# Loads of one batch with six in flight, and three smaller edits, in a gated linear attention fused with a ReGLU layer

## The chip, the cores and the metric

The kernel runs on one core of a Trainium2 chip. The metric is the device time of one execution in microseconds (us), as the median of several runs. The profiled execution is a separate run; its span, from the first to the last instruction, is a little shorter than the device time.

## The reference

Inputs q, k, v and f_logit have 4 batches, 8 heads, 768 positions and a head width of 48, in float32. The first half is a recurrence along the sequence, for each batch and head:

```
f = 1 / (1 + exp(-f_logit))
for t in range(768):
    state = f[t, :, None] * state + outer(k[t], v[t])     # 48 x 48
    y[t]  = q[t] @ state
```

The results of the heads are put side by side to a matrix x of 3072 x 384, and the second half is a feed-forward layer:

```
out = (relu(x @ w_gate) * (x @ w_val)) @ w_out            # 384 -> 1536 -> 384
```

## The kernel before

**Chunks.** The sequence is cut into 6 steps (c = 0 to 5) of 128 positions, and a step has 4 batches (b = 0 to 3). Within a step the recurrence becomes matrix products. For one batch of one step, from step 1 on, the work is this:

- `f_in` is loaded; ScalarE makes ln(1 + exp(-f)) of it in two passes, for two batches at a time (lines 572 and 575, the second writes `bneg`). So this pair of instructions needs the f of both batches.
- `cum` on TensorE: line 582 multiplies with a triangle of ones, which gives running sums of log decay; line 584 adds four one-column products that give the decay over the whole step. ScalarE makes `expo` of the sums (lines 591 and 593), and `dec` of the four columns (line 597, not in the last step).
- GpSimd multiplies k and q by `expo` into `hats` (lines 602 and 605) and turns v into `vpad` (line 558).
- `hats` is transposed into `qkT`: in steps 1 and 2 by TensorE (line 615, then a copy on VectorE, line 621), from step 3 on by a DMA that transposes (line 624).
- `scores` on TensorE (line 638), the mask on VectorE (line 644), the output products on TensorE (lines 673 and 677), a copy to `xn` on ScalarE (line 691). `xn` is transposed into `xT`: by TensorE (line 699, copy on VectorE, line 703) in steps below `first_xbar_x`, by a DMA (line 707) from there on.
- `state` (lines 718, 732 and 734) carries the state to the next step.

**Feed-forward.** For each step, line 766 makes the gate and value products for 12 blocks of hidden columns, 773 and 777 the ReLU and the product, line 789 the output product, 809 the copy to `osb`, and 812 the store.

**Who orders the work.** The kernel lists its operations with estimated durations and dependences, and a list scheduler (`Plan.schedule`) simulates the five engines and the DMA. At each turn it takes the operation that can start first, by priority where several can. The result is a fixed order of instructions on each engine; at run time each instruction waits for semaphores in that order. So an estimate that is off does not change the order: the engine stands and waits. Feed-forward products have a priority value 1000 higher than the attention's, so they are taken only where the plan sees no attention work ready. All loads, stores and transposing DMAs are issued by SyncE (SP) and stand in one order too.

**Loads.** `early` lists the loads of steps 0 and 1 and of the weights. From step 2 on a loop adds the loads in the order f, k, q, v for each group of `load_batches` batches. Each must wait until the load `flight` places earlier has landed:

```
for b in range(0, B, load_batches):
    for n in "fkqv":
        ...
        loads.append(load(n, c, b, b + load_batches, loads[-flight:][:1]))
```

A batch of one tensor and step is 192 KB, in rows of 192 bytes, so a load of two batches is 384 KB. The tiles for the loads are kept three times (`NL = 3`), so the loads of step c need the buffers of step c - 3.

Of the kernel before, what the change touches and what calls it, by code (L numbers as in the profile page):

```python
# [43 lines left out]
class Plan:  # L44
# [9 lines left out]
    def add(self, eng, emit, reads=(), writes=(), occ=0.5, lat=0.2, prio=0, opens=(), after=(), follows=(),  # L54
            paced=()):
        op = Op(eng, emit, list(reads), list(writes), occ, lat, prio, opens, after, follows, paced)
        op.idx = len(self.ops)
        self.ops.append(op)
        return op
# [169 lines left out]
def bass_hgrn2_outer__then__ffn_reglu_kernel(  # L229
# [13 lines left out]
             "wo2 f1.2.4 k1.2.4 q1.2.4 v1.2.4").split()  # L243
    lag = 4.0
    first_xbar_qk = 3
    flight = 3
    WP = 0
    NWARM = 100
    split_first = 1
# [1 line left out]
    spread_engines = ['ACT', 'DVE', 'ACT', 'ACT']  # L251
    load_engine = 'SP'
    n_tiled = 1
    first_xbar_x = 4
    load_batches = 2
    hat_engines = ['DVE', 'POOL']
    TAIL = [0, 256, 384]
    groups = [(0,0,4,1),(1,0,2,0),(1,2,4,0),(2,0,4,0),(3,0,4,0),(4,0,4,0),(5,0,4,0)]
    B, H, S, D = q.shape
    C = 128  # L260
    NC = S // C
    HD = H * D
# [3 lines left out]
    NP = H // 2  # L266
# [10 lines left out]
    bneg = [sb(f"bneg{i}", [128, 2, H, 64], BF16) for i in range(NB)]  # L277
# [168 lines left out]
    def chain(line, *args, **kw):  # L446

        last = tails.get(line)
        tails[line] = add(*args, follows=[last] if last else [], **kw)
        return tails[line]  # L450
# [95 lines left out]
    def attention(c, b):  # L546
# [14 lines left out]
        if c == 0:  # L561
            if b % 2 == 0:
                first_pair(b // 2)
            khat = khn[b % 2]
            kh_key = [f"khn{b % 2}"]
            back_transpose(b)
        else:
            parts = [(b, b + 2)] if b % 2 == 0 else []
            for b0, b1 in parts:
                fl = fin[:, b0:b1, :, :].rearrange("p b h d -> p (b h) d")  # L570
                keys = [f"f{li}_{x}" for x in range(b0, b1)]
                add("ACT", lambda: sc.activation(fl, fl, AF.Exp, scale=-1.0), keys, keys, prio=P,  # L572
                    **act_t((b1 - b0) * HD))
                bo = bneg[bi][:, b0 % 2:b0 % 2 + b1 - b0, :, 0:D].rearrange("p b h d -> p (b h) d")
                add("ACT", lambda: sc.activation(bo, fl, AF.Ln, bias=1.0), keys + [f"bneg{bi}"],
                    [f"bn{bi}_{x % 2}" for x in range(b0, b1)], prio=P, **act_t((b1 - b0) * HD))

            bn = bneg[bi][:, bj, :, :]
            bc = Bank("bc")

            def cum():
                te.matmul(bc.ap[:, 0:HD], tri[:, :], bn[:, :, 0:D])  # L582
                for p in range(NP):
                    mm = te.matmul(bc.ap[:, HD + p:HD + p + 1],  # L584
                                   bn[:, 2 * p:2 * p + 2, :].rearrange("p h d -> p (h d)"), ones[:, :])
                return mm
            chain("cum", "PE", cum, ["tri", "ones", f"bneg{bi}", f"bn{bi}_{bj}"], [bc], occ=0.29, lat=PE_L,
                prio=P, opens=[bc])

            ex = expo[ei]  # L590
            add("ACT", lambda: sc.activation(ex[:, 1, :], bc.ap[:, 0:HD], AF.Exp, scale=1.0), [bc],  # L591
                [f"expk{ei}"], prio=P + 1, **act_t(HD))
            add("ACT", lambda: sc.activation(ex[:, 0, :], bc.ap[:, 0:HD], AF.Exp, scale=-1.0), [bc],  # L593
                [f"expq{ei}"], prio=P + 1, **act_t(HD))
            if c < NC - 1:
                for j in range(2):
                    add("ACT", lambda lo=64 * j, j=j: sc.activation(dec[ai][lo:lo + 64, :, j], bc.ap[lo:lo + 64, HD:HD + NP],
                                                                    AF.Exp, scale=-1.0),
                        [bc, f"dec{ai}"], [f"dec{ai}_{j}"], prio=P + 2, **act_t(NP))

            hq, hk = hats[hi][:, 0, :, 0:D], hats[hi][:, 1, :, 0:D]
            add("POOL", lambda: gp.tensor_tensor(hk, kin[:, b, :, :], ex[:, 1, :].rearrange("p (h d) -> p h d", h=H),  # L602
                                                 ALU.mult),
                [f"k{li}_{b}", f"expk{ei}", f"hats{hi}"], [f"hk{hi}"], prio=P + 2, occ=0.95, lat=0.2)
            add("POOL", lambda: gp.tensor_tensor(hq, qin[:, b, :, :], ex[:, 0, :].rearrange("p (h d) -> p h d", h=H),  # L605
                                                 ALU.mult),
                [f"q{li}_{b}", f"expq{ei}", f"hats{hi}"], [f"hq{hi}"], prio=P + 2, occ=0.95, lat=0.2)
            if c < first_xbar_qk:
                tp = Bank("tp")

                def transposes():
                    t16 = tp.ap[:, :].bitcast(BF16)
                    for x in (1, 0):
                        for p in range(NP):
                            mm = te.transpose(t16[:, (x * NP + p) * C:(x * NP + p + 1) * C],  # L615
                                              hats[hi][:, x, 2 * p:2 * p + 2, :].rearrange("p h d -> p (h d)"), ident[:])
                    return mm
                chain("transposes", "PE", transposes, ["ident", f"hk{hi}", f"hq{hi}"], [tp], occ=pe_t(*[C] * 8), lat=PE_L, prio=P + 3,
                    opens=[tp])
                flat = qkT[qi].rearrange("p x n t -> p (x n t)")  # L620
                add("DVE", lambda: ve.tensor_copy(flat, tp.ap[:, :].bitcast(BF16)),
                    [tp], qk_key, prio=P + 4, **dve_t(512))
            else:
                op = add("SP", lambda: sy.dma_start(qkT[qi].rearrange("p x n t -> p (x n) t"),
                                                    hats[hi][:, :, :, :].rearrange("p x h d -> p (x h d)"), transpose=True),
                         [f"hk{hi}", f"hq{hi}"], qk_key, prio=P + 3, occ=1.2, lat=1.2)
                dma(op, f"qkT{qi}", 1.06, late)
                op.ring = "own" if load_engine == "ACT" else "SP"
            khat = hats[hi][:, 1, :, :].rearrange("p h d -> p (h d)")
            kh_key = [f"hk{hi}", f"hats{hi}"]  # L630
# [149 lines left out]
    def ffn_out(g, *bs):  # L780

        gi = g % NG
        cuts = TAIL if (g, bs[-1]) == (NC - 1, B - 1) else [0, DM]
        parts = [(b, n0, n1, Bank("f")) for b in bs for n0, n1 in zip(cuts, cuts[1:])]

        def proj_out(o, b, s, n0, n1):
            def run():
                for j in range(s * OJ, (s + 1) * OJ):
                    mm = te.matmul(o.ap[:, 0:n1 - n0], gT[gi][:, j, b * C:(b + 1) * C], wo[:, j, n0:n1],  # L789
                                   start=(j == 0), stop=(j == NJ - 1))  # L790
                return mm
            return run

        def rows(b, n0, n1, o, s):
            js = range(s * OJ, (s + 1) * OJ)
            P = (g + 1) * B * 10 + 5 + NJ * 3 + b * 3
            chain("ffn", "PE", proj_out(o, b, s, n0, n1), [f"gT{gi}_{j}_{b}" for j in js] + sorted({f"wo{j // WJ}" for j in js}),
                  [o], occ=pe_t(*[n1 - n0] * OJ), lat=PE_L, prio=P + 1000, opens=[o] if s == 0 else [])
        if len(cuts) > 2:
            for part in parts:  # L800
                for s in range(NJ // OJ):
                    rows(*part, s)
        else:
            for s in range(NJ // OJ):
                for part in parts:
                    rows(*part, s)
        for b, n0, n1, o in parts:
            oi, P = (g * B + b) % NO, (g + 1) * B * 10 + 5 + NJ * 3 + b * 3
            add("ACT", lambda o=o, oi=oi, n0=n0, n1=n1: sc.activation(osb[oi][:, n0:n1], o.ap[:, 0:n1 - n0], AF.Copy), [o], [f"osb{oi}_{x}" for x in TAIL[:-1] if n0 <= x < n1],  # L809
                prio=P, **act_t(n1 - n0))  # L810
            dst = bass.AP(tensor=out.tensor, offset=(b * S + g * C) * DM + n0, ap=[[DM, C], [1, n1 - n0]])
            op = add("SP", lambda dst=dst, oi=oi, n0=n0, n1=n1: sy.dma_start(dst, osb[oi][:, n0:n1]), [f"osb{oi}_{x}" for x in TAIL[:-1] if n0 <= x < n1], [f"out{g}_{b}_{n0}"],
                     occ=0.2, lat=0.9, prio=P)
            dma(op, f"osb{oi}_{n0}", 0.45 * (n1 - n0) / DM)

    OJ = 4
    OPAIR = 2
    count = {"h": 0}
# [44 lines left out]
                n += 1  # L863
            op.val = n

    stores = [op for op in order["SP"] if op.writes and op.writes[0].startswith("out")]

    def run(name, eng):
        for op in order[name]:
# [63 lines left out]
```

## Time and profile before

| what | value |
|---|---|
| device time | median of 3 runs 203.14 us (202.06 to 204.03) |
| span of the profiled run | 201.4 us |
| TensorE busy | 191.7 us, 95% of the span |
| ScalarE, VectorE, GpSimd busy | 115.2, 107.9 and 77.3 us |
| bytes moved by DMA | 31.35 MB, 156 GB/s over the span |
| DMA issues of loads after step 1 | 32 of 384 KB |
| DMA issues that transpose | 12 of qkT, 8 of xT |

The page gives the busy share of each engine in 40 slices of about 5 us. The chain of waits follows the work that ended last back from the last instruction. The view of windows gives busy time, the granted TensorE clock and the share of the DMA engines in stretches that one chooses; a share above 1 means that packets of several transfers lay over each other. The timeline of SP shows its DMA issues; such an issue contains its own wait for semaphores[...].

### The profile page before, as it was taken

How to read it: one execution, taken by the hardware profiler on the slowest of the kernel's cores; microseconds unless marked ns; L12 is line 12 of the kernel's file. 1: busy time of each engine (PE TensorE's matmuls, PEld its weight loads, DVE VectorE, ACT ScalarE, POOL GpSimd, SP SyncE). 2: the span in 40 equal slices, each digit the busy share in tenths (PEclk: the TensorE clock that was granted, in tenths of full speed). 3: DMA queues.
4: the chain of work that ended last, by engine and by line, in shares of the span. 5: the costliest groups of instructions: out<-in, count | busy, mean ns of one | idle time of the engine just before them, and what ended most of it. 6: DMA issues, size and time to landing. Idle time of an engine off the chain costs nothing.

```text
span 201.4 us, 4570 instructions
## 1 busy us (share of the span) xinstructions
PE 191.7 (95%) x1813; PEld 124.4 (62%) x1813; DVE 107.9 (54%) x212; ACT 115.2 (57%) x264; POOL 77.3 (38%) x111
## 2 busy tenths in 40 slices
PE   7989899799999999999999999599999999999995
PEld 5766688676789787855664655245555555444564
DVE  7268575565098988628586846135462334433210
ACT  2976868716678686877677572744354333443412
POOL 5189203563559687772858364053000000000000
PEclk9999999999999999999999999969999999999999
DMA  4999999999999999999989998979222001111113
GB/s 119 234 223 196 198 200 180 204 231 210 230 232 232 158 247 189 221 198 230 192 161 234 159 199 186 189 156 221 77 63 59 24 19 39 39 39 42 39 39 117
DMA packets 116660, 31.35 MB, mean 156 GB/s; under 512 B 109600, under 2 KB 116640, under 8 KB 116640
## 3 DMA queue, kind: packets, MB, share of 16 engines
q1 hardware_dynamic: 112656, 27.53, 67.2%
q0 software_dynamic: 3984, 3.54, 11.0%
q8 instruction: 14, 0.23, 0.5%
q14 instruction: 6, 0.05, 0.1%
HBM read 25.95 MB, written 4.72 MB: 152 GB/s over the span
## 4 chain that ended last, share of the span: by engine, by line
PE 73%; DMA 13%; SPq 8%; ACT 2%; POOL 2%; issue 1%; DVE 0%
PE ps L766 37%; PE ps L789 22%; SPq L399 7%; DMA q_in<-in_q_dram 4%; DMA wv<-in_moe_w_val_dram 4%; PE ps L638 3%; DMA f_in<-in_f_logit_dram 3%; DMA v_in<-in_v_dram 3%; PE ps L615 2%; PE ps L677 2%; PE ps L582 2%; PE ps L673 2%; PE ps L718 1%; PE ps L699 1%; PE ps L584 1%
## 5 line engine op out<-in xcount | busy, mean ns | idle before, releaser
L777 DVE TENSOR_TENSOR gT<-relu,ps 128x256 bf16<-128x256 bf16 (+1 forms) x96 | 52.2, 552 | 59.9 <-PE ps L766 37.2
L766 PE MATMUL ps<-xT,wg 128*128 128x256 bf16 (+1 forms) x288 | 63.1, 328 | 0.3 <-DMA wg<-in_moe_w_gate_dram 0.3
L773 ACT ACTIVATE relu<-ps 128x256 bf16<-128x256 f32 (+1 forms) x96 | 46.3, 490 | 29.1 <-PE ps L766 28.7
L766 PE MATMUL ps<-xT,wv 128*128 128x256 bf16 (+1 forms) x288 | 62.6, 326 | 0.0
L789 PE MATMUL ps<-wo,gT 128*128 128x384 bf16 (+2 forms) x300 | 52.5, 320 | 0.0
L789 PEld LDWEIGHTS ps<-wo,gT 128*128 128x128 bf16 x300 | 27.7, 98 | 17.4
L766 PEld LDWEIGHTS ps<-xT,wg 128*128 128x128 bf16 x288 | 27.0, 98 | 15.6 <-DMA wg<-in_moe_w_gate_dram 0.6
L644 DVE TENSOR_TENSOR ptm<-ps,tri 128x512 bf16<-128x512 f32 x48 | 30.6, 684 | 10.8 <-PE ps L638 10.7
L766 PEld LDWEIGHTS ps<-xT,wv 128*128 128x128 bf16 x288 | 26.1, 98 | 16.0 <-ACT relu L773 0.2
L809 ACT ACTIVATE osb<-ps 128x384 f32<-128x384 f32 (+2 forms) x25 | 11.8, 477 | 30.6 <-PE ps L789 30.5
L602 POOL TENSOR_TENSOR hats<-k_in,expo 128x384 bf16<-128x384 f32 x20 | 20.0, 1000 | 20.3 <-ACT expo L591 20.3
L605 POOL TENSOR_TENSOR hats<-q_in,expo 128x384 bf16<-128x384 f32 x20 | 20.0, 1002 | 2.2 <-DMA q_in<-in_q_dram 2.2
L734 POOL TENSOR_TENSOR st<-ssum,dec 128x384 bf16<-128x384 f32 x16 | 13.3, 830 | 16.2 <-DVE ssum L732 16.2
L455 PE MATMUL ps<-zeros 128*128 128x256 bf16 x89 | 13.0, 301 | 1.1 <-DVE zeros L359 1.1
L691 ACT ACTIVATE xn<-ps 128x384 bf16<-128x384 f32 x20 | 9.8, 488 | 7.1 <-PE ps L677 7.1
L558 POOL CAST vpad<-v_in 128x384 bf16<-128x384 f32 x24 | 12.0, 515 | 3.0 <-DMA v_in<-in_v_dram 2.8
L572 ACT ACTIVATE f_in<-f_in 128x768 f32<-128x768 f32 x10 | 8.4, 838 | 6.4 <-DMA f_in<-in_f_logit_dram 6.4
L591 ACT ACTIVATE expo<-ps 128x384 f32<-128x384 f32 x20 | 9.8, 492 | 3.0 <-PE ps L584 2.9
L455 PEld LDWEIGHTS ps<-zeros 128*128 128x128 bf16 x89 | 9.0, 107 | 3.0 <-DVE zeros L359 1.1
L638 PE MATMUL ps<-qkT 48*128 48x128 bf16 x192 | 8.9, 226 | 1.2 <-ACT qkT L528 0.8
L593 ACT ACTIVATE expo<-ps 128x384 f32<-128x384 f32 x20 | 10.0, 498 | 0.0
L732 DVE TENSOR_TENSOR ssum<-ps,st 128x384 f32<-128x384 f32 x16 | 8.8, 551 | 1.1 <-PE ps L718 0.9
(71 smaller groups left out, 158.3 us busy)
## 6 DMA issues: line engine op xcount, KB each, us to landing
out_dram<-osb SPq DMA_DIRECT2D x23, 192.0 KB, 2.2
f_in<-in_f_logit_dram SPq DMA_DIRECT2D x10, 384.0 KB, 6.2
k_in<-in_k_dram SPq DMA_DIRECT2D x10, 384.0 KB, 6.4
q_in<-in_q_dram SPq DMA_DIRECT2D x10, 384.0 KB, 4.5
v_in<-in_v_dram SPq DMA_DIRECT2D x10, 384.0 KB, 4.8
wg<-in_moe_w_gate_dram POOLq DMA_DIRECT2D x3, 384.0 KB, 7.1
wv<-in_moe_w_val_dram POOLq DMA_DIRECT2D x3, 384.0 KB, 7.4
wo<-in_moe_w_out_dram POOLq DMA_DIRECT2D x3, 384.0 KB, 7.2
```

What stands on the lines that cost most here:

```text
L399: op = add(eng, lambda: e.dma_start(dst, src), [], [f"{n}{c % NL}_{b}" for b in range(b0, b1)], occ=(0.8 if eng == "SP" else 0.3) * (b1 - ...
L455: op = add("PE", lambda: te.matmul(cold.ap[:, 0:256], zeros[:, 0:128], zeros[:, :]), ["zeros"], [cold], occ=0.22 if i < 17 else 0.11, lat= ...
L558: add("POOL", lambda: gp.tensor_copy(vout, vin[:, b, :, :].rearrange("p (n j) d -> p n j d", j=2)), [f"v{li}_{b}", f"vpad{vi}"], [f"v_{vi} ...
L602: add("POOL", lambda: gp.tensor_tensor(hk, kin[:, b, :, :], ex[:, 1, :].rearrange("p (h d) -> p h d", h=H), ALU.mult), [f"k{li}_{b}", f"ex ...
L605: add("POOL", lambda: gp.tensor_tensor(hq, qin[:, b, :, :], ex[:, 0, :].rearrange("p (h d) -> p h d", h=H), ALU.mult), [f"q{li}_{b}", f"ex ...
L638: mm = te.matmul(s.ap[:, p * C:(p + 1) * C], qkT[qi][lo:lo + D, 1, p, :], qkT[qi][lo:lo + D, 0, p, :])
L644: add("DVE", lambda j=j, s=s: ve.tensor_tensor(ptm[mi][:, j, :, :], s.ap[:, :].rearrange("p (n t) -> p n t", n=NP), mask, ALU.mult), [s, " ...
L734: add("POOL", lambda: gp.tensor_tensor(t4(s_new), t4(tmp), rate, ALU.mult), [key] + dk, [f"S{b}_{c % 2}"], prio=P + 8, **pool_t(HD))
L766: mm = te.matmul(bank.ap[:, 0:n], wt[:, kt, j * 128:(j + 1) * 128], xT[xi][:, kt, n0:n1], start=(kt == 0), stop=(kt == NK - 1))
L773: add("ACT", lambda: sc.activation(relu[ri][:, 0:n], gate.ap[:, 0:n], AF.Relu), [gate], [f"relu{ri}"], prio=P, **act_t(n))
L777: add("DVE", lambda: ve.tensor_tensor(gT[gi][:, j, n0:n1], relu[ri][:, 0:n], val.ap[:, 0:n], ALU.mult), [val, f"relu{ri}"], [f"gT{gi}_{j}_ ...
L789: mm = te.matmul(o.ap[:, 0:n1 - n0], gT[gi][:, j, b * C:(b + 1) * C], wo[:, j, n0:n1], start=(j == 0), stop=(j == NJ - 1))
```

## The change

Four constants or conditions change what the kernel does; the rest of the diff adds options that keep their old meaning (`STORE = 'SP'` leaves the stores where they were, and `first_stores` is empty).

- `load_batches` 2 to 1: from step 2 on a load brings one batch (192 KB). The order becomes f, k, q, v of batch 0, then of batch 1, and so on.
- `flight` 3 to 6: a load waits for the one six places earlier, so that again six batches at most are under way. It is to keep the DMA evenly busy with smaller pieces.
- `first_xbar_x` 4 to 3: the four transposes of x in step 3 move from TensorE and VectorE to DMAs on SP.
- In step 5 the four one-column products of `cum` are left out, since no later step uses the decay. The plan's estimate for `cum` is lowered by 0.12 there.

```diff
-    flight = 3
+    flight = 6
...
-    first_xbar_x = 4
-    load_batches = 2
+    first_xbar_x = 3
+    load_batches = 1
     hat_engines = ['DVE', 'POOL']
+    STORE = 'SP'
...
             def cum():
-                te.matmul(bc.ap[:, 0:HD], tri[:, :], bn[:, :, 0:D])
-                for p in range(NP):
+                mm = te.matmul(bc.ap[:, 0:HD], tri[:, :], bn[:, :, 0:D])
+                for p in range(NP if c < NC - 1 else 0):
                     mm = te.matmul(bc.ap[:, HD + p:HD + p + 1],
                                    bn[:, 2 * p:2 * p + 2, :].rearrange("p h d -> p (h d)"), ones[:, :])
                 return mm
-            chain("cum", "PE", cum, ["tri", "ones", f"bneg{bi}", f"bn{bi}_{bj}"], [bc], occ=0.29, lat=PE_L,
+            chain("cum", "PE", cum, ["tri", "ones", f"bneg{bi}", f"bn{bi}_{bj}"], [bc], occ=0.29 - (0.12 if c == NC - 1 else 0), lat=PE_L,
                 prio=P, opens=[bc])
...
-            op = add("SP", lambda dst=dst, oi=oi, n0=n0, n1=n1: sy.dma_start(dst, osb[oi][:, n0:n1]), [f"osb{oi}_{x}" for x in TAIL[:-1] if n0 <= x < n1], [f"out{g}_{b}_{n0}"],
-                     occ=0.2, lat=0.9, prio=P)
+            op = add(STORE, lambda dst=dst, oi=oi, n0=n0, n1=n1: (sy if STORE == "SP" else sc).dma_start(dst, osb[oi][:, n0:n1]), [f"osb{oi}_{x}" for x in TAIL[:-1] if n0 <= x < n1], [f"out{g}_{b}_{n0}"],
+                     follows=first_stores if g == 0 else [], occ=0.2 if STORE == "SP" else 0.4, lat=0.9 if STORE == "SP" else 1.2, prio=P)
```

More of the change, by code (lines that the diff above doesn't have):

```diff
@@ L811, in ffn_out @@
             dst = bass.AP(tensor=out.tensor, offset=(b * S + g * C) * DM + n0, ap=[[DM, C], [1, n1 - n0]])
-            op = add("SP", lambda dst=dst, oi=oi, n0=n0, n1=n1: sy.dma_start(dst, osb[oi][:, n0:n1]), [f"osb{oi}_{x}" for x in TAIL[:-1] if n0 <= x < n1], [f"out{g}_{b}_{n0}"],
-                     occ=0.2, lat=0.9, prio=P)
+            op = add(STORE, lambda dst=dst, oi=oi, n0=n0, n1=n1: (sy if STORE == "SP" else sc).dma_start(dst, osb[oi][:, n0:n1]), [f"osb{oi}_{x}" for x in TAIL[:-1] if n0 <= x < n1], [f"out{g}_{b}_{n0}"],
+                     follows=first_stores if g == 0 else [], occ=0.2 if STORE == "SP" else 0.4, lat=0.9 if STORE == "SP" else 1.2, prio=P)
             dma(op, f"osb{oi}_{n0}", 0.45 * (n1 - n0) / DM)
+    first_stores = [tails["loadSP"]] if '0' == "1" else []
     OJ = 4
@@ L864, in bass_hgrn2_outer__then__ffn_reglu_kernel @@
             op.val = n
-    stores = [op for op in order["SP"] if op.writes and op.writes[0].startswith("out")]
+    stores = [op for op in order[STORE] if op.writes and isinstance(op.writes[0], str) and op.writes[0].startswith("out")]
     def run(name, eng):
```

## The prediction

> **What bounds the kernel now.** I read the 40 slices first: they show whether TensorE (PE) has holes.
>
> ```profile
> PE   7989899799999999999999999599999999999995
> ...
> PEclk9999999999999999999999999969999999999999
> DMA  4999999999999999999989998979222001111113
> ```
>
> PE is full from slice 8 (40 us) to the end, but for one slice, number 25 (126 to 131 us), with a 5. In the slice after it the granted clock is at 6. The DMA engines are about full until slice 26. So PE sets the time, and the DMA stands close behind it for the first 136 us. The part up to 40 us (loads of steps 0 and 1 and of the weights) belongs to lines that the change does not touch, so I leave it as it is. The windows around the hole come next; columns are the window, its length, PE, PEld, DVE, ACT and POOL busy, the granted clock, the DMA share and GB/s.
>
> ```profile
> 116.00:122.00 6.00, 5.71 (x59) 3.08 (x55) 3.13 (x5) 3.34 (x8) 4.46 (x5) 1.00 1.01 215
> 122.00:127.00 5.00, 5.00 (x46) 2.74 (x45) 2.10 (x4) 1.09 (x2) 1.09 (x3) 1.00 0.68 129
> 127.00:130.00 3.00, 0.81 (x8) 0.29 (x7) 0.69 (x1) 2.73 (x6) 0.00 (x0) 1.00 1.33 229
> 130.00:135.00 5.00, 5.00 (x40) 2.52 (x39) 1.25 (x2) 3.21 (x8) 2.08 (x3) 0.66 0.94 194
> ```
>
> PE is idle 2.19 us in 127 to 130. After that 5 us run at a mean clock of 0.66, which costs 0.34 x 5 = 1.7 us. Just before, in 122 to 127, the DMA was at 0.68 and 129 GB/s: it had too little to do, right before PE waited for a load. The chain of waits says which load.
>
> ```profile
> 118.80 0.61 ACT relu L773
> 119.42 1.22 SPq L812
> 120.68 1.19 SPq L707
> ...
> 121.92 5.33 DMA f_in<-in_f_logit_dram
> 127.27 0.84 ACT f_in L572
> ...
> 128.98 0.74 ACT bneg L575
> ...
> 129.76 0.34 PE ps L582
> ```
>
> This is f of batches 2 and 3 of step 5, the last of the f loads. It is issued at 121.92, lands 5.33 us later, goes through two ScalarE passes, and `cum` (line 582) stands first in PE's order. PE has 60 us of feed-forward products left, but behind that instruction. Why was it issued so late? SP's timeline:
>
> ```profile
> 115.71 2.42 SPq L624 DMA_TRANSPOSE qkT<-hats  x1
> 118.17 0.58 SPq L399 DMA_DIRECT2D v_in<-in_v_dram  x1
> 118.80 1.84 SPq L812 DMA_DIRECT2D out_dram<-osb  x1
> 120.68 1.19 SPq L707 DMA_TRANSPOSE xT<-xn  x1
> 121.92 0.58 SPq L399 DMA_DIRECT2D f_in<-in_f_logit_dram  x1
> ```
>
> SP's order puts it behind a transpose, a store (1.84 us, with a wait for ScalarE) and another transpose. The limit of three in flight did not hold it: SP waits for loads to land for 1.3 us in all between 40 and 140 us. What holds it is its place in the order, which comes from the plan, where the limit does count.
>
> **What the Trainium skill says.** "DMA: Bandwidth & Descriptors", Anatomy of one DMA, says that DMA engines do not wait on semaphores; the issuing sequencer does before dispatch. The trace agrees: the DMA lull follows SP's waits. The same page, Bandwidth, advises DMAs of at least 1 MiB, and its section "Why small descriptors are slow" blames the size of the single row. Halving a load here leaves rows at 192 bytes, so I take no loss of rate; no run here shows it yet. "TensorE: Matmul & The Clock Gate", Part 1, gives half clock after an idle window of about 3.4 us. Here 2.19 us of idle was enough for 5 us at 0.66, so the loss is real for shorter holes, and it should go when the hole goes.
>
> **The change part by part.**
>
> *Decay columns of step 5.* Four times, the four products of line 584 leave PE. The chain gives 0.08 to 0.10 us for each four. Removed: about 0.35 us of PE. Nothing reads them, since line 597 is skipped in that step.
>
> *Transposes of x in step 3.* Off PE: four groups of three (line 699) at 0.17 to 0.20 us in the chain, about 0.7 us. Off VectorE: four copies of 0.35 us, hidden, since VectorE is busy 54%. Onto SP: four transposing DMAs.
>
> ```profile
> L707 SPq DMA_TRANSPOSE xT<-xn x8: 1179/1250/2088, 120.7 to 150.5; - x8
> ```
>
> The issue costs SP at least 1.18 us each, so about 4.8 us of SP, between about 95 and 108 us, where SP has work all the time. Behind them in SP's order stand loads of steps 4 and 5 and the qkT transposes, and `cum` and `scores` wait for those. In DMA time each is small: the window 150 to 160 has a queue share of 15.1%, and stores alone (six in 160 to 190 at 9.0%) cost 0.45 us each, which leaves (1.51 - 0.9) / 2 = 0.3 us. x also reaches `xT` about 2.4 us after issue in place of some 0.7 us through PE and VectorE. The feed-forward products of step 3 wait for it; products of step 2 lie before them and hide it if the plan orders it so. Bounds on the path: 0, and 4.8 us if SP is what sets the loads.
>
> *Loads of one batch.* 32 issues become 64. The freest issues of 384 KB take 0.37 to 0.58 us, and the single-batch ones at the start 0.63 us. From 50 us on the 32 take 41 us together, which I read as mostly waiting for room in the queue. Even 64 x 0.63 = 40 us fits in that, so I cost the issues at nothing[...]. DMA pace: 221 GB/s in 50 to 75 us gives 0.89 us for 192 KB.
>
> *The order of pieces.* Before, the f pair of batches 2 and 3 is complete after 10 of the step's 16 pieces of 192 KB; after the change, with f3 behind f2, k2, q2 and v2, after 13. That is 3 x 0.89 = 2.7 us later for the same start. Against it: k, q and v of batch 2 are then already there, and the plan knows the new order, so it places `cum` later too.
>
> *Six in flight.* In the plan, a load of one batch is assumed to land sooner than one of two, so it releases the next sooner, and loads come earlier in SP's order against stores and transposes. The bytes under way stay the same. This is what can fill the lull at 122 to 127 (5 us at 0.68: 1.6 us of DMA time) and take f out from behind the store.
>
> **Sum for the forecast.** 203.14 - 2.2 (the wait) - 1.7 (the clock) - 1.05 (PE work) = 198.2. A new fixed order seldom fits without any wait: other waits of PE after 40 us in the trace run from 0.3 us (scores on qkT) to 1.5 us (transposes on `hats`). I add 1.0, between 0 and the present 2.2: 199.2.
>
> **The rivals.**
>
> *B, the hole stays.* The DMA is about full from 40 to 120 us (share 1.01 to 1.16), so loads cannot come much earlier whatever the plan believes. If f still comes too late by some 2 us, with the clock loss after it, only the PE work goes, and what goes ahead of the hole only widens it. That gives 203.14 - 1.05 = 202.1 to 203.0; I say 202.5. For it: the DMA share. Against it: the lull at 0.68 right where it hurts.
>
> *C, slower.* The four transposes on SP (4.8 us) and the later place of the f pair (2.7 us) delay the attention of steps 4 and 5 beyond what the plan assumes. At the full 7.5 us nothing hides it, and 203.14 - 1.05 + 7.5 = 209.6; half of it, 3.75, gives 205.8. For it: SP has hardly a gap between 95 and 122 us, and its in-order waits already caused this hole. Against it: the plan knows these costs at about their size, and PE has enough feed-forward products to put ahead of `cum`.
>
> **How the numbers follow.** The hole and the lull stand side by side, and the change rearranges just that queue, so I give the forecast 0.57. B gets 0.23, C 0.20. The forecast lies at 198 to 201, all of it below 201.1 (1% faster); B lies within 1%; C above 205.2. Hence faster 0.57, same 0.23, slower 0.20. The range starts at 197.3, the sum without any new wait less half a per cent for the spread of the runs. It ends at 204.5, past B and its spread, leaving out most of C.
>
> **What would show it.** Right: no 5 in the PE slices near 126 us, PEclk at 9 throughout, no wait of `cum` on `bneg` above 1 us, 24 products of line 699 in place of 36, 12 transposes of line 707, and a DMA share without a lull before the last f load. Wrong: a PE hole of 2 us or more after 90 us followed by a lower clock (B), or several such holes, or SP waiting in line 707 with loads behind it (C). The forecast fails if the loads turn out to be bound by DMA bandwidth and not by their place in the order.

## The result and the profile after

The changed kernel is slower: 212.65 us (211.42 to 214.41) against 203.58 us of before, a ratio of 1.046 with a 95% interval of 1.039 to 1.054. Here and below, ratios leave out slow runs, those over 1.5% above the fastest of their kernel, and medians count all, so a ratio is not always the quotient of two medians. The profiled run has a span of 211.3 us, 9.9 us more than before. Lines have moved by one, so `cum` is lines 583 and 585 and the transposing DMA of x is line 708. The 40 slices of the kernel after:

```profile
PE   7988899699998979899789894999999999999995
...
PEclk9999999999999999999999998799999999999999
DMA  5999999999999899999959799888522111111113
```

Before, PE had one hole after 40 us. Now seven slices from 12 to 24, counted from 0, are not full. The DMA row hardly differs but for single slices (an 8, a 5, a 7). The windows say how much; the columns are as in the prediction.

```profile
40.00:50.00 10.00, 8.51 (x95) 6.14 (x96) 6.24 (x12) 2.52 (x6) 5.39 (x8) 1.00 1.15 207
...
70.00:80.00 10.00, 8.58 (x120) 6.39 (x115) 5.88 (x14) 6.66 (x19) 6.01 (x8) 1.00 0.96 194
...
100.00:110.00 10.00, 8.76 (x88) 5.03 (x86) 6.50 (x11) 5.68 (x16) 5.98 (x8) 1.00 0.98 172
110.00:120.00 10.00, 7.80 (x64) 3.90 (x64) 4.87 (x8) 6.38 (x17) 5.63 (x7) 1.00 0.84 172
120.00:130.00 10.00, 6.99 (x57) 3.77 (x56) 2.51 (x6) 3.85 (x8) 1.29 (x2) 1.00 1.00 182
```

Added up over the eleven windows from 40 to 150 us (PE is busy 10.00, 9.39, 9.02, 9.50, 9.73 and 9.63 us in the six that are not shown), PE is idle 12.1 us; the same windows of before give 3.1 us. The difference, 9.0 us, is the loss. The clock is not part of it: it is 0.83 in 130 to 140 us and 1.00 in the other windows, in both kernels.

ScalarE's timeline shows where the wait begins: line 573, the first pass over an f pair, for five of the six pairs of steps 3 to 5.

```profile
76.33 0.84 ACT L573 ACTIVATE f_in<-f_in 128x768 f32<-128x768 f32 x1 [1.92 <-DMA f_in<-in_f_logit_dram]
85.61 0.84 ACT L573 ACTIVATE f_in<-f_in 128x768 f32<-128x768 f32 x1 [2.70 <-DMA f_in<-in_f_logit_dram]
97.16 0.84 ACT L573 ACTIVATE f_in<-f_in 128x768 f32<-128x768 f32 x1 [1.62 <-DMA f_in<-in_f_logit_dram]
108.98 0.84 ACT L573 ACTIVATE f_in<-f_in 128x768 f32<-128x768 f32 x1 [2.37 <-DMA f_in<-in_f_logit_dram]
127.13 0.84 ACT L573 ACTIVATE f_in<-f_in 128x768 f32<-128x768 f32 x1 [5.54 <-DMA f_in<-in_f_logit_dram]
```

The brackets give ScalarE's idle time and what ended it: a load of f, each time. Before, the last pair of step 5 was passed at 127.27 us; now only the first pair of step 5 is, at 127.13, and the last at 138.34. SP's timeline ahead of the 5.54 us wait:

```profile
104.15 1.28 SPq L400 DMA_DIRECT2D f_in<-in_f_logit_dram  x1
105.47 4.13 SPq L708 DMA_TRANSPOSE xT<-xn  x2
109.65 0.58 SPq L400 DMA_DIRECT2D k_in<-in_k_dram  x1
...
113.15 1.79 SPq L625 DMA_TRANSPOSE qkT<-hats  x1
114.99 0.58 SPq L400 DMA_DIRECT2D f_in<-in_f_logit_dram  x1
115.61 2.55 SPq L708 DMA_TRANSPOSE xT<-xn  x2
...
123.78 0.58 SPq L400 DMA_DIRECT2D f_in<-in_f_logit_dram  x1
```

The f pieces of batches 0 and 1 of step 5 are issued at 114.99 and 123.78 us. Between them and before them stand the four new transposes of x (6.7 us of SP), qkT transposes, a store, and k, q and v of batch 0.

### The profile page after: what moved, and what is told of

It reads as the page before. It is cut to its first block, busy times and chain, and to the rows that moved or that the text cites. A ratio compares the mean times of both kernels' runs of the same rounds, so it can differ in the third digit from the quotient of the medians.

```text
span 211.3 us, 4574 instructions
## 1 busy us (share of the span) xinstructions
PE 192.6 (91%) x1785; PEld 123.3 (58%) x1785; DVE 106.5 (50%) x208; ACT 114.8 (54%) x264; POOL 76.8 (36%) x111
## 4 chain that ended last, share of the span: by engine, by line
PE 46%; SPq 20%; DMA 20%; ACT 8%; issue 3%; POOL 1%; DVE 1%; DVEq 0%
PE ps L767 24%; PE ps L790 18%; SPq L400 17%; DMA f_in<-in_f_logit_dram 9%; DMA q_in<-in_q_dram 4%; DMA wv<-in_moe_w_val_dram 4%; ACT relu L774 3%; DMA v_in<-in_v_dram 3%; ACT bneg L576 1%; SPq L625 1%; PE ps L639 1%; ACT f_in L573 1%; SPq L813 1%; SPq L708 1%; ACT xn L692 1%
## 5 line engine op out<-in xcount | busy, mean ns | idle before, releaser
L767 PEld LDWEIGHTS ps<-xT,wv 128*128 128x128 bf16 x288 | 26.7, 98 | 18.0 <-ACT osb L810 1.3
L559 POOL CAST vpad<-v_in 128x384 bf16<-128x384 f32 x24 | 12.1, 507 | 36.3 <-DMA v_in<-in_v_dram 26.3
L592 ACT ACTIVATE expo<-ps 128x384 f32<-128x384 f32 x20 | 9.9, 495 | 5.2 <-PE ps L585 3.4
L639 PEld LDWEIGHTS ps<-qkT 48*128 48x128 bf16 x192 | 5.8, 97 | 8.6 <-issue 5.1
L583 PE MATMUL ps<-bneg,tri 128*128 128x384 bf16 x20 | 6.8, 338 | 4.0 <-ACT bneg L576 3.9
```

Of the source, the lines that this page charges most:

```text
L559: add("POOL", lambda: gp.tensor_copy(vout, vin[:, b, :, :].rearrange("p (n j) d -> p n j d", j=2)), [f"v{li}_{b}", f"vpad{vi}"], [f"v_{vi} ...
L639: mm = te.matmul(s.ap[:, p * C:(p + 1) * C], qkT[qi][lo:lo + D, 1, p, :], qkT[qi][lo:lo + D, 0, p, :])
L767: mm = te.matmul(bank.ap[:, 0:n], wt[:, kt, j * 128:(j + 1) * 128], xT[xi][:, kt, n0:n1], start=(kt == 0), stop=(kt == NK - 1))
```

## The experiments

**The theories.** Theory 1: the loads come much as before, but the plan takes them to come sooner, and so fixes an order in which attention work stands ahead of its data. Theory 2: the four new transposes hold up SP and the loads behind them. Theory 3: the f pair is complete only with the fifth piece. Theory 4: small issues cost by themselves. Each group of kernels ran beside runs of before on the same chip; before took 200.79 us in the first group, 200.61 in the second and 203.76 in the third, so ratios are compared, not times. (A part of what sets these medians apart stands in the last section.)

### One part at a time

```diff
-    flight = 3
+    flight = 6
...
-    load_batches = 2
+    load_batches = 1
```

> Only the loads are changed (one batch, six in flight); x of step 3 and the decay columns stay as before. Theory 1 (the plan takes the small loads to land sooner than they do, so cum stands too early in PE's order): most of the 9 us stays, 209 to 213 us, with PE waits of cum on bneg of several us in all. Theory 2 (the four transposes of step 3 on SP hold up the loads): 203 to 205 us. Theory 3 (the f pair is complete only with the fifth piece): as theory 1, 209 to 213 us.

Measured: 211.19 us, ratio 1.056 (1.048 to 1.063). The loads alone bring the whole loss, so theory 2 is not needed for it. The waits of PE are not those of `cum` on `bneg` that I expected: this trace puts none down to lines 582 and 584. They come at many other instructions of the attention, the longest (2.8 us) at line 673.

```diff
-    first_xbar_x = 4
+    first_xbar_x = 3
```

> Only x of step 3 goes to the transposing DMA; loads as before. Theory 1 and 3: 202 to 204.5 us, 0.7 us of PE work less and small new waits. Theory 2: 209 to 213 us, SP waiting in line 707 between 95 and 110 us with loads behind it.

Measured: 205.43 us, ratio 1.026 (1.021 to 1.031). Smaller than theory 2 said, but real, and not hidden as theories 1 and 3 said. SP's and PE's timelines of this run, and one of its windows:

```profile
97.63 5.17 SPq L707 DMA_TRANSPOSE xT<-xn  x2
...
109.65 4.03 SPq L707 DMA_TRANSPOSE xT<-xn  x2
113.73 0.58 SPq L399 DMA_DIRECT2D f_in<-in_f_logit_dram  x1
```

```profile
111.53 0.34 PE L673 MATMUL ps<-st,qkT 128*128 128x96 bf16 x4 [1.39 <-DVE ptm L644]
...
114.87 1.46 PE L766 MATMUL ps<-xT,wg 128*128 128x512 bf16 x3 [2.79 <-DMA xT<-xn]
```

```profile
115.00:120.00 5.00, 4.78 (x30) 2.67 (x30) 1.71 (x3) 1.92 (x3) 1.03 (x3) 0.50 0.89 176
```

The two pairs of transposes hold SP for 9.2 us, their waits included (above all for ScalarE, which writes `xn`), and the loads stand behind them: the first f pair of step 5 is passed at 119.16 us, before at 113.27. PE waits 2.79 us for `xT` itself, and the next product takes 1.46 us in place of the usual 0.81: the clock is at half. From 40 to 150 us PE is idle 6.0 us, where the profile of before has 3.1. The clock of 0.84, 0.50 and 0.98 in the three windows of 5 us from 110 to 125 us costs another 3.4 us, estimated as the clock loss was in the prediction. So more than half of the some 5 us lost here is clock.

```diff
-                for p in range(NP):
+                for p in range(NP if c < NC - 1 else 0):
...
-            chain("cum", "PE", cum, ["tri", "ones", f"bneg{bi}", f"bn{bi}_{bj}"], [bc], occ=0.29, lat=PE_L,
+            chain("cum", "PE", cum, ["tri", "ones", f"bneg{bi}", f"bn{bi}_{bj}"], [bc], occ=0.29 - (0.12 if c == NC - 1 else 0), lat=PE_L,
```

> Only the sixteen one-column products of step 5 are left out. All theories: 203.58 less 0.2 to 0.4 us, so 203.2 us, which three rounds can't tell from no change; more than 1 us in either direction would mean that the order of the plan alone moves the time.

Measured: 203.07 us, ratio 1.011 (1.004 to 1.019). The expected 203.2 us is met by luck only, since before took 200.79 us in this group. Sixteen tiny products less, and not faster. The hole of 2.1 us at `cum` is there as before. Three of the four runs had a mean granted clock below 1.0 (0.992, 0.983, 0.992), but only two of the eight of before; the one at 1.0 took 201.11 us, among the 199.57 to 201.8 us of before at 1.0. So the 1.1% goes along with the lower clock, and nothing in these runs shows a gain; whether the slightly changed order has a part in it, they don't tell.

### Is it the plan's belief?

Only the estimate of when a load lands is changed, in the kernel after:

```diff
+    LATER = 6.0
...
-        dma(op, f"{n}{c % NL}_{b0}{b1}", flow, (6.0 if (c, n, b0) == (1, "v", 0) else 2.0) if c else 0.8)
+        dma(op, f"{n}{c % NL}_{b0}{b1}", flow, (6.0 if (c, n, b0) == (1, "v", 0) else 2.0 + (LATER if c > 1 else 0)) if c else 0.8)
```

> The kernel after, but the plan is told that a load of step 2 and later lands 6.0 us later than it assumed; no instruction is added or removed, only the fixed order can change. Theory 1: at least two thirds of the loss is gone, 202 to 206 us, and the PE waits of cum on bneg fall below 1 us. Theory 2 and 3: the loads still come late on SP, 209 to 213 us.

Measured: 230.88 us, ratio 1.154 (1.144 to 1.163). A miss, against all theories. I had overlooked that the same estimate paces the loads in the plan: a load starts there when the one six places earlier is taken to have landed. So the loads went far back in SP's order. A window of this run (the last two columns are DMA share and GB/s):

```profile
80.00:100.00 20.00, 14.71 (x126) 9.21 (x126) 8.14 (x15) 9.84 (x26) 11.26 (x14) 0.66 0.72 140
```

From 60 to 120 us the DMA moves 137 to 140 GB/s, where it had about 200: it has too little to do. So this run can't tell the theories apart, but it shows that the estimate must not be too late either. The loads alone, with an estimate 1.7 us later, which gives six pieces the planned time of three loads of two batches:

```diff
-        dma(op, f"{n}{c % NL}_{b0}{b1}", flow, (6.0 if (c, n, b0) == (1, "v", 0) else 2.0) if c else 0.8)
+        dma(op, f"{n}{c % NL}_{b0}{b1}", flow, (6.0 if (c, n, b0) == (1, "v", 0) else 2.0 if c == 1 else 3.7) if c else 0.8)
```

> As the run with the loads alone, but the plan is told that a load lands 1.7 us later, which gives six pieces the same planned time as three loads of two batches had. No instruction is added or removed. Theory 1: most of the loss gone, 201 to 205 us. Theory 3: the pieces keep their order, so no more than a third of the loss goes, 207 to 211 us.

Measured: 202.57 us, ratio 1.008 (1.005 to 1.011), from 1.056. The instructions, the pieces and the six in flight are the same; five sixths of the loss is gone with one constant of the plan. Its slices:

```profile
PE   7988899989999999989999999988999999999995
```

The loads don't come sooner for it. ScalarE's first pass over the two f pairs of step 5, with the loads alone and then in this run:

```profile
119.87 0.84 ACT L572 ACTIVATE f_in<-f_in 128x768 f32<-128x768 f32 x1 [4.89 <-DMA f_in<-in_f_logit_dram]
132.37 0.84 ACT L572 ACTIVATE f_in<-f_in 128x768 f32<-128x768 f32 x1 [0.69 <-DMA f_in<-in_f_logit_dram]
```

```profile
118.95 0.84 ACT L572 ACTIVATE f_in<-f_in 128x768 f32<-128x768 f32 x1 [0.81 <-DMA f_in<-in_f_logit_dram]
133.17 0.84 ACT L572 ACTIVATE f_in<-f_in 128x768 f32<-128x768 f32 x1 [2.08 <-DMA f_in<-in_f_logit_dram]
```

Each of the four waited for f, so these are the times at which f landed: within 1 us of each other. For all loads of steps 2 to 5, the landings in this run lie between 2.1 us before and 3.2 us after those of the loads alone, with a median of 0.6 us before. Yet PE is idle 4.0 us from 40 to 150 us in place of 10.5. So the loss lies in the order in which the engines take their work, and not in when the loads arrive. By the plan's own durations, 71.7 us of feed-forward products stand ahead of the `cum` of the last f pair in PE's order with the loads alone, and 81.4 us in this run: PE has other work while that f is on its way.

The other side, loads of two batches as before and a plan that takes them to come sooner:

```diff
-    flight = 3
+    flight = 6
```

> Before, with loads of two batches and flight 6 in place of 3; the chip hardly waited for that limit, so only the plan changes, which takes the last loads to be issued much earlier. Theory 1: slower than before by 2% or more, 205 to 212 us, with f landing later than the plan set cum for. Theory 3: within 1% of before.

Measured: 207.62 us, ratio 1.033 (1.027 to 1.039). The last v load is issued in this run at

```profile
124.31 1.36 SPq L399 DMA_DIRECT2D v_in<-in_v_dram  x1
```

and in the kernel before at 134.66 us. So the loads do come sooner, by 10 us at the end, and the kernel is slower. The plan expects them sooner still: it takes the last f pair to land at 113.1 us, and it is passed at 121.14.

The kernel's scheduler computes, while the program is built, when the plan takes each load to land. The table sets the start of the first pass over each f pair of steps 2 to 5 in the trace against that planned landing; positive means later than planned, in us. The pass can start later than the data, so these are upper bounds of the lag.

| kernel | lag of the eight pairs | ratio |
|---|---|---|
| before | 1.8, 1.6, 0.2, 0.8, 0.9, 0.7, 0.9, 4.0 | 1 |
| after | 2.2, 3.0, 4.2, 5.9, 7.3, 9.3, 13.6, 14.8 | 1.046 |
| loads alone | 2.1, 2.3, 3.4, 5.4, 6.5, 8.1, 10.9, 12.1 | 1.056 |
| two batches, flight 6 | 2.3, 1.4, 2.7, 3.2, 5.0, 5.3, 6.8, 8.0 | 1.033 |
| loads alone, 1.7 us later | 1.3, -1.6, -0.9, -1.2, -1.0, -0.5, -0.6, 1.6 | 1.008 |

The planned spacing of the f pairs is 9.8 us before ((123.3 - 54.7) / 7) and 9.1 us with the new loads; the traces have 10.1 and 10.5 us. In these five kernels, where the lag grows, the kernel is slow. The lag arises before the issue of a load, not behind it: with the loads alone, the last f is issued at 129.27 us where the plan has 115.7, and lands 3.1 us later, where the plan allows 4.6. So what is off in the plan is the pace of the loads. The later estimate slows that pace in the plan to 10.4 us for an f pair, and the trace of that run has 10.5.

### The pieces themselves

The loads alone, in pair order:

```diff
-        for b in range(0, B, load_batches):
-            for n in "fkqv":
+        for b2 in range(0, B, 2):
+            for n, b in [(n, b) for n in "fkqv" for b in (b2, b2 + 1)]:
```

> As the run with the loads alone (211.19 us), but the pieces come in pair order: f of batches 0 and 1, then k, q and v of both, still 192 KB each with six in flight. The plan again takes loads to land soon. Theory 1 (plan too optimistic): 206 to 212 us, since the plan sets cum still earlier. Theory 3 (the f pair is complete only with the fifth piece, three pieces or some 2.7 us later): back to within 1% of before, 199 to 203 us.

Measured: 208.79 us, ratio 1.040 (1.034 to 1.046). The last f pair now passes at 125.20 us, sooner than before's 127.27, and still most of the loss stays, with a lag that grows from 2.3 to 9.5 us. So the place of the fifth piece can be a part (1.6 of the 5.6 points here) and not the main one: the run with the later estimate keeps that place and loses 0.8%.

The plan and the order of before, with each load issued as two DMAs:

```diff
+            def emit():
+                for b in range(b0, b1):
+                    ins = e.dma_start(t[:, b, :, :], bass.AP(tensor=srcs[n].tensor, offset=b * H * S * D + c * C * D,
+                                                             ap=[[D, C], [S * D, H], [1, D]]))
+                    if b < b1 - 1:
+                        ins.then_inc(op.sem, 16)
+                return ins
```

> Before with its plan and so its order on every engine, but each load of two batches from step 2 on is issued as two DMAs of 192 KB, one behind the other. Theory 4 (small issues themselves cost: SP time or DMA rate): 205 to 211 us. Theories 1 and 3: within 1% of before.

Measured: 202.20 us, ratio 1.008 (1.005 to 1.012), within 1% but a little slower. The issues of f in this run, as the view of the line gives them (minimum, median and maximum in ns):

```profile
L402 SPq DMA_DIRECT2D f_in<-in_f_logit_dram x16: 453/988/2055, 50.3 to 122.2; - x16
```

So 64 issues of 192 KB fit where 32 of 384 KB stood; the last v is issued at 134.7 us, as before. Theory 4 explains some 0.8%, and 1.2% at the upper end of the interval.

### The whole change with the mended estimate, and a faster kernel

The estimate of 3.7 in place of 2.0, the same edit as above, now in the kernel after:

> The kernel after, whole, with the plan told that a load lands 1.7 us later; no instruction is added or removed. Theory 1 alone: most of the 4.6% goes, 201 to 205 us. If the transposes of x in step 3 cost as much beside well estimated loads as they did alone (2.6%): 206 to 209 us.

Measured: 207.80 us, ratio 1.029 (1.022 to 1.037), so the second case. With the loads well estimated, what remains is about the price of the transposes alone (1.026). Is that price again an estimate that is off? The kernel with x of step 3 by DMA alone, and a later estimate for those transposes:

```diff
-                dma(op, f"xT{xi}_{b}", 0.4, late)
+                dma(op, f"xT{xi}_{b}", 0.4, late + (3.0 if c == 3 else 0))
```

> As the run with x of step 3 by DMA alone (205.43 us), with the plan told that those transposes land 3.0 us later. If the feed-forward products stand too early in PE's order: the PE wait on xT goes, 200 to 203 us. If the transposes hold up SP and so the loads behind them (theory 2): 204 us or more, f of step 5 still late.

Measured: 206.56 us, ratio 1.024 (1.016 to 1.032). No: the wait on `xT` is gone, and another has come in its place, on `vpad` and so on a v load. That load is issued at 108.17 us, behind the first two transposes, and lands at 115.08; before, it was issued at 106.33 and landed at 111.04. PE's timeline:

```profile
115.69 0.50 PE L718 MATMUL ps<-vpad,hats 128*128 128x96 bf16 x4 [3.36 <-POOL vpad L558]
```

The kernel before has one pair with a large lag in the table, the last (4.0 us), and one hole, at that pair. So the estimate of the loads of step 5 is set 3.0 us later, in before:

```diff
-        dma(op, f"{n}{c % NL}_{b0}{b1}", flow, (6.0 if (c, n, b0) == (1, "v", 0) else 2.0) if c else 0.8)
+        dma(op, f"{n}{c % NL}_{b0}{b1}", flow, (6.0 if (c, n, b0) == (1, "v", 0) else 5.0 if c == 5 else 2.0) if c else 0.8)
```

> Before, with the plan told that the loads of step 5 land 3.0 us later. Theory 1: the PE wait of cum on bneg before 130 us and the half clock after it go, 198 to 200 us against some 200.6 of before on the same chip. If the wait only moves elsewhere: 200 to 203 us.

Measured: 199.46 us, ratio 0.988 (0.982 to 0.993). All six runs (199.06 to 200.03 us) also lie below those runs of before in the group that had a clock of 1.0 (200.94 to 203.09 us). It is one group on one chip: in the second group, before itself had runs down to 199.30 us. The windows of this run at the place of the old hole:

```profile
122.00:127.00 5.00, 5.00 (x46) 2.73 (x45) 3.05 (x5) 3.66 (x8) 2.85 (x4) 1.00 0.85 170
127.00:130.00 3.00, 3.00 (x19) 1.59 (x17) 0.69 (x1) 1.12 (x3) 0.00 (x0) 1.00 1.22 264
130.00:135.00 5.00, 5.00 (x47) 2.67 (x46) 3.64 (x6) 3.63 (x8) 0.99 (x1) 1.00 0.52 103
```

PE is full and the clock whole. The f pair itself is passed at 129.27 us, 2 us later than before. The data did not come sooner; PE no longer stands waiting for it.

The same with the decay columns of step 5 left out, as in the edit of `cum` above:

> As the run with later loads in step 5, and without the decay columns of step 5. Theory 1: 0.3 us below that run, 197.7 to 199.7 us. If the plan's order shifts by chance as it did in the run without decay columns alone (1.1% slower): 200 to 203 us.

Measured: 199.06 us, ratio 0.986 (0.979 to 0.992). It is the fastest, but the 0.4 us to the run above lie within the spread of either.

## Why the prediction was wrong

I forecast 199.2 us and the time is 212.65; it is the side of rival C, past the end of my range.

- **What bounds the kernel before** was read rightly: one hole of about 2 us, a loss of clock after it, and `cum` waiting for the last f pair. The run with later loads in step 5 took just that hole away and came to 199.46 us.
- **The step that failed** is "Six in flight": "In the plan, a load of one batch is assumed to land sooner than one of two, so it releases the next sooner, and loads come earlier in SP's order". That is what the plan assumed, and it is the cause of the loss: I took the plan's belief for a gain on the chip. From 50 to 120 us the DMA moved 204 GB/s with the loads alone and 206 before, at a share of 1.04 and 1.06, so the stream was no faster, and the last f pair of the loads alone passes at 132.37 us where the plan takes it to land at 120.3. The order was fixed by that belief, and PE waits. The run with the estimate 1.7 us later shows it: the same landings, and the loss down from 5.6% to 0.8%. Nor do sooner loads help where the belief runs ahead of them: two batches with flight 6 bring the last load 10 us sooner, and the kernel is 3.3% slower.
- **"The plan knows the new order, so it places `cum` later too"**, in *The order of pieces*, is true by the plan's own clock and was no protection, since that clock is off by up to 15 us. For rival C I wrote that "the plan knows these costs at about their size". The table shows that it does not.
- **The transposes of x.** I bounded them by 0 and 4.8 us and took 0 for the forecast. Alone they cost 2.6%, some 5 us (1.026 of 200.79). That this meets the upper bound is luck: the 4.8 us were the bare issues, and SP stood 9.2 us in these transposes, its waits included, which I had left out; and by the estimate above 3.4 us of the loss are half clock, which I had not counted at all. That loads come later behind them is right. The 0.7 us of PE work was gone (24 products of line 700 in place of 36) and does not show.
- **The issues** at nothing: nearly right, some 0.8%. They don't quite fit in the old 41 us: in the split run SP spends 52 us on the 64 issues.
- **The decay columns**: the 0.35 us did not show in a run of the edit alone.
- **Rival C** had the side and part of the mechanism. Its delay of the f pair, at most 7.5 us, was too small: the last f pair passes 11 us later. I halved it because I trusted the plan to hide the rest.
- **Rival B** had said that the DMA is about full, "so loads cannot come much earlier whatever the plan believes". I did not ask what a plan does that believes it nevertheless: it opens new holes.

What the parts give does not add up: loads 1.056 and transposes 1.026 alone, 1.046 together. Why the two overlap is open. That the order and not the arrival of the loads makes the loss is shown for the loads alone, by the two runs with the same landings. An estimate shifts the order of PE, ScalarE, VectorE, GpSimd and SP together, though, and what each of them has of the loss is open.

## What to carry to other kernels

Where a planner writes a fixed order, a change of buffer counts or piece sizes changes first what the planner believes. Compare its planned landings with the trace; where the lag grows from step to step, the order doesn't fit the chip, and loads that come 10 us sooner did not mend it here. An estimate that also paces the loads must be right in both directions: 1.7 us more left 0.8% of a loss of 5.6%; 6 us more, in the whole changed kernel, turned 4.6% into 15%. Transposing DMAs on the queue that issues the loads hold up the loads behind them: four of them held SP for 9.2 us here, and an f pair behind them came 5.9 us later.

## What was not expected of the hardware

- Halving loads from 384 to 192 KB, with rows of 192 bytes, left the rate unchanged: 210 GB/s from 50 to 120 us with the split issue, 206 before, in a stretch in which both still have loads to come. The Trainium skill, "DMA: Bandwidth & Descriptors", Bandwidth, advises at least 1 MiB; between these two sizes, both below that, the trace shows no difference; no run here has 1 MiB.
- A wait of PE of about 2 us is followed by half clock in some runs and not in others. In the profile of before, 2.19 us were followed by a clock of 0.66 over 5 us. In the run in pair order, 2.3 us were not: the view of PE's waits (us in total, times, the longest) and a window with the clock in its third column from the right:

```profile
PE ps L766 <- ACT relu L773: 2.3, 1, 2.3
```

```profile
48.00:142.00 94.00, 85.88 (x940) 56.61 (x937) 56.80 (x110) 61.77 (x155) 55.30 (x69) 1.00 1.03 201
```

That wait ends at 104.59 us, within the window. In the first group, runs of before with a mean granted clock of 1.0 took 199.57 to 201.8 us, those with 0.992 took 203.19 and 203.42. The Trainium skill, "TensorE: Matmul & The Clock Gate", Part 1, says that the window in which the clock gate watches PE runs free, so that the moment of the change varies; that would fit, but no run here shows it. The kernel without that hole ran at 1.0 in all six runs, 199.06 to 200.03 us.
